# Attention's bias and threshold by one-column operations, gating's factors in PSUM, and the split sums of x in one block

## The chip, the cores and the metric

The kernel runs on one core of one Trainium2 chip. The metric is the device time of one execution in microseconds, the median over several runs. A core has five engines with instruction queues of their own, each worked off in order: TensorE (PE, matmuls), VectorE (DVE), ScalarE (ACT), GpSimd (POOL) and SyncE (SP, which issues most DMAs here). [...] Data lies in SBUF, and matmuls write to PSUM, which has 8 banks.

## The reference

Three computations in a row, all in float32:

```
scores = q @ k.T / 8                        # batch 2, 8 heads, 576 rows, head size 64
scores = where(scores >= max(scores) - tau, scores, -1e9)
attn   = exp(scores - max(scores));  attn /= sum(attn) + 1e-9
x      = attn @ v                           # as 1152 tokens of 512

P = exp(x @ w_gate - max(x @ w_gate))       # 1152 x 8 experts
8 times:  P /= P.sum(1) + 1e-9;  P /= P.sum(0) + 1e-9;  P *= 1152 / 8
x = sum over 8 experts e of  P[:, e] * (relu(x @ w1[e]) @ w2[e])      # hidden size 1024

p = domain_probs / (its row sums + 1e-9)
out = sum over 4 experts e of  p[:, e] * (relu(x @ w1[e]) @ w2[e])
```

The softmax's threshold is taken at the row's own maximum; with `tau` at or above zero the row maximum always stays in.

## The kernel before

**Number format.** Matmuls run on float32 operands that are split in two parts, a rounded `hi` and a remainder `lo`, with three matmuls for one product (lo by hi, hi by lo, hi by hi). A split is one cast on ACT for `hi` and one subtraction on DVE or POOL for `lo`. Splits are done for q, k, v, the weights (names `wh` and `wl`; POOL does the subtraction), x (`xh` and `xl`), the hidden rows (`hh`/`hl`, `hs`) and certain sums of x (`xth` and `xtl`).

**Order.** The program is written out in the order in which each engine is to execute it; the framework adds the semaphores. Three stretches follow each other.

*Attention* (up to some 260 us). 72 units of 128 score rows go through a software pipeline. In one `step`, `scores` of unit t+2 (PE, line 270, 261 for the first ones), `top` of unit t+1 (DVE, row maximum, line 275), `mask` of unit t (DVE, line 287), `guard` (line 291), `line` of unit t+1 (line 279) and `norm` (a reciprocal on DVE, line 295, and a scaling on POOL, line 297) stand in this order; then the transposes of an older unit (PE, line 305), the copy of its transposed rows (ACT, line 312), the exponential of unit t+1 (ACT, line 283), the low part `etl` of the transposed rows (DVE, line 322), and the products with v (PE, lines 340 to 349). `line` makes from the row maximum two columns of the small tile `st`: column 1 is the bias of the exponential, column 2 the threshold of the mask. With m the maximum, `lin` the constants:

```
st[:, 1:3] = lin[:, 0:2] * m - lin[:, 2:4]
lin[:, 0:2] = (-0.125 if tau >= 0 else 0, 1)        lin[:, 2:4] = (0, 8 tau, or a huge number if tau < 0)
```

Between these, PE is given matmuls of the first two experts on the tokens that are ready (`expert_fill`, lines 460 and 488, with DVE's `hl` at line 469 and small copies on POOL). How many of them a step gets is written into the program and does not depend on times.

*Rest of the fill, and gating* (some 260 to 352 us). A loop pulls three pieces of `expert_fill` at a time and between them one piece of a generator: `gate` (lines 709 to 746) at every third turn, and `sums(1)` or `scale` (line 753) in the other turns. `gate` makes the logits, the exponential and then the 8 rounds of normalising `p1`, a tile of 128 rows x 72 numbers (9 token tiles of 8 experts). In a round DVE sums over experts into `rs` (line 731), adds 1e-9 (732), inverts (733) and multiplies `p1` by it (734); PE sums over the rows with a matrix of ones (line 737); DVE sums that over the tiles into `cs` (738), adds, inverts and multiplies (739 to 741). `sums(c)` makes, for one half of the tokens, the sums of column blocks of x that the next layers read (lines 772 to 781) and their splits (line 71 on ACT, line 76 on DVE). Its last six splits go to the tiles `xth` and `xtl`, for which there is room only when the fill's weights are no longer needed; so the generator pauses there.

*The mixtures in half-size blocks* (from 352 us to the end). `layer1` (line 885, 14 slots of six matmuls, ACT and DVE work at lines 860, 861, 890 to 909) and `layer2` (line 989, with the sums into `acc` at line 997) alternate over half experts and halves of the tokens. After each slot `tick` is called: it advances the preparation of the next weights by one piece (`cook1`, `cook2`: a cast on ACT and a subtraction on POOL, at most one every two ticks), and it advances by one piece the first generator of the list `behind`. Whatever remains of a half's generator in `pending` is worked off in `drain`, just before the slots of `layer1` that read `xth` and `xtl` (the fifth slot and on). A slot's matmuls write to a bank that an earlier slot may have filled; the fifth and sixth slot write to those that `s` (line 890) was copied from. After the first `layer1`, `sums(0)` begins, for the other half of the tokens.

PSUM banks of the last two stretches come from one pool of eight, `bank()`.

Of the kernel before, what the change touches and what calls it, by code (L numbers as in the profile page):

```python
# [9 lines left out]
F32 = mybir.dt.float32  # L10
F32R = mybir.dt.float32r
AF = mybir.ActivationFunctionType
ALU = mybir.AluOpType
# [5 lines left out]
E1, E2 = 8, 4  # L19
P = 128  # L20
KT = DM // P
FT = F // P
NT = N // P
# [6 lines left out]
def attention_two_moe_kernel(ctx, tc, qP, kP, qT, kT, vp, tau, wg, w1, w1s, w2, dp, m2w1s, m2w2, out):  # L30
    nc = tc.nc
    V, A, G, T = nc.vector, nc.scalar, nc.gpsimd, nc.tensor
# [4 lines left out]
    def pool(stack, name, bufs=1, **kw):  # L37
        return stack.enter_context(tc.tile_pool(name=name, bufs=bufs, **kw))

    cp = pool(ctx, "const")  # L40
# [13 lines left out]
    tau_sb = cp.tile([P, 1], F32, name="tau_sb")  # L54
    warm = cp.tile([P, 1], F32, name="warm")
    A.activation(warm, ones[:, 0:1], AF.Exp)
    esc = cp.tile([P, 1], F32, name="esc")
    lin = cp.tile([P, 4], F32, name="lin")
    on = cp.tile([P, 1], F32, name="on")
    wg_sb = cp.tile([P, KT, E1], F32, name="wg_sb")  # L60
    wg2 = cp.tile([P, KT, 2 * E1], F32R, name="wg2")
# [7 lines left out]
    def split(eh, el, hi, lo, src):  # L69
        if eh is A:  # L70
            A.copy(hi, src)  # L71
        elif eh is V:
            V.tensor_copy(hi, src)
        else:
            G.tensor_scalar(hi, src, 1.0, 1.0, op0=ALU.mult, op1=ALU.mult)
        el.tensor_tensor(lo, src, f(hi), op=ALU.subtract)  # L76
# [6 lines left out]
    def fetch(n):  # L83
        while len(raws) < n and tiles:
            w, e, ft = tiles.pop(0)
            raw = rp.tile([P, DM], F32, tag="raw", name="raw", bufs=3)
            nc.sync.dma_start(raw, w[e, :, ft])
            raws.append(raw)
# [22 lines left out]
    class Attention:  # L111
# [164 lines left out]

        def line(self, u):
            st = u["st"]
            V.scalar_tensor_tensor(st[:, 1:3], lin[:, 0:2], st[:, 0:1], lin[:, 2:4], op0=ALU.mult, op1=ALU.subtract)  # L279

        def exp(self, u):
            ex = u["ex"] = self.pl.tile([P, 2, HS], F32, tag="ex", name="ex", bufs=4)
# [163 lines left out]
    def bank():  # L446
        return banks.tile([P, 512], F32, tag="mm", name="mm")
# [60 lines left out]
    with ExitStack() as att:  # L508
        ap = pool(att, "attn", side="right")
        ps_s = pool(att, "ps_s", 2, space=PSUM)  # L510
        ps_t = pool(att, "ps_t", 1, space=PSUM)
        ps_r = pool(att, "ps_r", 1, space=PSUM)
        banks.pool = ps = pool(att, "ps_m", 2, space=PSUM)
        at = Attention(ap, ps_s, ps_t, ps_r, ps)
        for p in range(H // 2):
            at.add_pair(0, p, 0, 256, True, p == 0)
        nA0 = len(at.units)
        for p in range(H // 2):
            at.add_pair(0, p, 256, 320, False)
        nA1 = len(at.units)  # L520
        for p in range(H // 2):
            at.add_pair(1, p, 0, S, False)
        at.plan()
        room = [2 * FT]
        at.load()
        G.memset(lin, 0.0)
        G.memset(lin[:, 1:2], 1.0)
        V.tensor_scalar(on, tau_sb, 0.0, None, op0=ALU.is_ge)
        V.tensor_scalar(esc, on, 0.125, None, op0=ALU.mult)
        V.tensor_scalar(lin[:, 0:1], on, -0.125, None, op0=ALU.mult)  # L530
        V.tensor_scalar(on, on, -BIG, BIG, op0=ALU.mult, op1=ALU.add)
        V.scalar_tensor_tensor(lin[:, 3:4], tau_sb, 8.0, on, op0=ALU.mult, op1=ALU.add)

        def side():
            if at.t >= -1:
                fetch(2)
            if at.t >= nA0 - 3 and raws and room[0] and (at.t < nA1 or room[0] > 2 or at.t % 2):
                room[0] -= 1
                cook()
            if at.t == 20:  # L540
                nc.sync.dma_start(wg_sb, wg)
                nc.sync.dma_start(dp_sb, dp)
            if at.t == 24:
                split(V, V, wg2[:, :, :E1], wg2[:, :, E1:], wg_sb)

        def free(n):
            room[0] += n

        X0, X1 = Expert(0), Expert(1)
        near, far = ((0, 0), (1, P)), ((2, 32), (3, 32 + P))  # L550
        todo = [(nA0 + 3, expert_fill(hp, X0, 0, 256, near, acc, None, 0, at.later, keep)),
                (nA1 + 3, expert_fill(hp, X0, 256, 320, far, acc, tail0[0], 0, at.later, free)),
                (nA1 + 3, expert_fill(hp, X1, 0, 256, near, y1, None, 0, at.later, keep)),
                (nA1 + 3, expert_fill(hp, X1, 256, 320, far, y1, tail0[1], 0, at.later, keep))]

        left, spent = [0], [0]

        def pull(n, end=True):

            for i in range(n):  # L560
                if not todo or at.t <= todo[0][0] or (left[0] == 1 and not end):
                    return i
                left[0] = next(todo[0][1], -1)
                if left[0] < 0:
                    todo.pop(0)
                if left[0] <= 0:
                    left[0] = 0
                    return i + 1
            return n

        def fill(phase, busy):
            if phase == 0:
                if 0 <= at.t < nA0 - 3:
                    room[0] -= 1
                    cook(None if at.t % 2 else at.later)
                spent[0] = pull(3)
            elif left[0] or not busy:
                pull(max((RA1 if at.t < nA1 + 3 else RA2) - spent[0], 0), True)

        while at.step(fill, side):  # L580
            pass
        at.flush()
        while left[0]:
            pull(1)
        at.flush()
        while raws:
            cook()
            fetch(2)
# [25 lines left out]
    gp = pool(ctx, "gate", side="right", reuse_waits="tile")  # L614
# [61 lines left out]
    behind = []  # L676
# [26 lines left out]
    def gate():  # L703
        lt = gp.tile([2 * E1, N], F32, name="lt")
        for q in range(4):
            lg = bank()
            for i, x in enumerate((xl, xh)):
                for kt in range(KT):
                    T.matmul(lg[:2 * E1, :HS], lhsT=wg2[:, kt], rhs=x[:, kt, q * HS:(q + 1) * HS],
                             start=i == 0 and kt == 0, stop=i == 1 and kt == KT - 1)  # L710
            A.copy(lt[:, q * 2 * P:(q + 1) * 2 * P], lg[:2 * E1, :2 * P])
            A.copy(lt[:, 8 * P + q * 32:8 * P + (q + 1) * 32], lg[:2 * E1, 2 * P:HS])
            yield 1
        pl = bank()
        for t in range(NT):
            T.matmul(pl[:, t * E1:(t + 1) * E1], lhsT=lt[:, t * P:(t + 1) * P], rhs=both[:2 * E1], start=True, stop=True)
        A.copy(p1.rearrange("p t e -> p (t e)"), pl[:, :NT * E1])
        gm = gp.tile([P, 4], F32, name="gm")
        V.tensor_reduce(gm[:, 0:1], p1, axis=AX.XY, op=ALU.max)
        yield 1  # L720
        pm, pn = bank(), bank()
        T.transpose(pm[:1, :P], gm[:, 0:1], ident)
        V.tensor_reduce(gm[:1, 1:2], pm[:1, :P], axis=AX.X, op=ALU.max)
        yield 1
        T.matmul(pn[:, 0:1], lhsT=ones[:1, :], rhs=gm[:1, 1:2], start=True, stop=True)
        V.tensor_scalar(gm[:, 2:3], pn[:, 0:1], -1.0, None, op0=ALU.mult)
        A.activation(p1, p1, AF.Exp, bias=gm[:, 2:3])
        rs = gp.tile([P, NT], F32, name="rs")
        cs = gp.tile([P, E1], F32, name="cs")
        for _ in range(8):  # L730
            V.tensor_reduce(rs, p1, axis=AX.X, op=ALU.add)
            V.tensor_scalar(rs, rs, 1e-9, None, op0=ALU.add)
            V.reciprocal(rs, rs)
            V.tensor_tensor(p1, p1, rs[:, :, None].to_broadcast([P, NT, E1]), op=ALU.mult)
            yield 1
            pc = bank()
            T.matmul(pc[:, :NT * E1], lhsT=ones, rhs=p1.rearrange("p t e -> p (t e)"), start=True, stop=True)
            V.tensor_reduce(cs, pc[:, :NT * E1].rearrange("p (t e) -> p e t", t=NT), axis=AX.X, op=ALU.add)
            V.tensor_scalar(cs, cs, 1e-9, None, op0=ALU.add)
            V.reciprocal(cs, cs)  # L740
            V.scalar_tensor_tensor(p1, p1, float(N) / E1, cs[:, None, :].to_broadcast([P, NT, E1]),
                                   op0=ALU.mult, op1=ALU.mult)
        V.tensor_reduce(rs, dp_sb, axis=AX.X, op=ALU.add)
        V.tensor_scalar(rs, rs, 1e-9, None, op0=ALU.add)
        V.reciprocal(rs, rs)
        V.tensor_tensor(p2, dp_sb, rs[:, :, None].to_broadcast([P, NT, E2]), op=ALU.mult)
        yield 1
# [55 lines left out]
    gt, s1, sl = gate(), sums(1), scale()  # L803
# [21 lines left out]
    hp = pool(ctx, "hs", reuse_waits="tile")  # L825
    tp = pool(ctx, "temps", reuse_waits="tile")
    pending = [None, s1]
    behind += [s1, gt, sl]

    def begin(c, work):  # L830
        pending[c] = chain(pending[c] or (), work)
# [240 lines left out]
```

## Time and profile before

| | us |
|---|---|
| median of 3 runs | 1394.73 (1394.54 to 1398.56) |
| the profiled execution | 1393.83 |
| its span, from the first to the last instruction | 1392.0 |
| PE busy | 1331.3 (96%) |
| DVE busy | 710.0 (51%) |
| POOL busy | 662.0 (48%) |
| ACT busy | 560.9 (40%) |

Durations come from one profiled execution. A row of the timeline has the start in us from the beginning of the span, the duration in us, engine, line of the program, operation, the tiles that it writes and reads, shapes and the count of merged instructions; in brackets stands the idle time of the engine ahead of it and what ended that time. A matmul's row is longer than its share of PE's time, since the next one starts before it has ended: times of PE are read from start to start. Times of DVE are read in the same way where short operations follow each other.

### The profile page before, as it was taken

The page shows a single profiled execution, that of the slowest core. Times are in us where ns is not written, and L with a number is a line of the kernel's source. Part 1 is how long each engine was busy: PE and PEld are TensorE (multiplying, and loading weights), DVE is VectorE, ACT ScalarE, POOL GpSimd, SP SyncE. Part 2 cuts the span into 40 slices and gives each one's busy share as a digit, 9 for nine tenths or more (in the row PEclk, how much of TensorE's full clock was granted, in tenths as well). Part 3 has the DMA queues.
Part 4 walks back from the last instruction along what each step waited for, and adds up shares of the span by engine and source line. Part 5 has one row for each costly group of instructions (what it writes and reads, how often), then busy time and mean ns, then how long its engine had stood idle before and what let it go on. Part 6 is the DMA issues. An engine that isn't in the chain of part 4 may idle for free.

```text
span 1392.0 us, 21443 instructions
## 1 busy us (share of the span) xinstructions
PE 1331.3 (96%) x8089; PEld 1191.5 (86%) x8089; DVE 710.0 (51%) x1579; ACT 560.9 (40%) x1286; POOL 662.0 (48%) x792
## 2 busy tenths in 40 slices
PE   7788999999889999999999999999899999999998
PEld 4578898889779898988889898988788989888887
DVE  6799999555654333343434343435653434334343
ACT  5767677421444242333323242423442424233331
POOL 5766777351565354345335443542433543453330
PEclk9999999999999999999999999999999999999999
DMA  5522231010221111111111011101011101111101
GB/s 164 154 83 78 77 97 44 24 31 9 72 73 54 46 51 34 54 46 31 54 40 60 24 53 47 58 26 46 24 46 46 61 24 54 46 38 47 31 8 61
DMA packets 42055, 73.61 MB, mean 53 GB/s; under 512 B 5088, under 2 KB 10336, under 8 KB 41952
## 3 DMA queue, kind: packets, MB, share of 16 engines
q1 hardware_dynamic: 41664, 71.96, 17.2%
q8 instruction: 64, 1.05, 0.3%
q14 instruction: 39, 0.32, 0.1%
q10 hardware_dynamic: 288, 0.28, 0.1%
HBM read 69.86 MB, written 2.36 MB: 52 GB/s over the span
## 4 chain that ended last, share of the span: by engine, by line
PE 76%; DVE 14%; ACT 5%; issue 2%; POOL 2%; DMA 0%; DVEq 0%; ACTq 0%; POOLq 0%
PE mm L989 37%; PE mm L885 29%; PE mm L488 4%; DVE ex L287 2%; PE mm L460 2%; DVE st L275 2%; DVE st L279 1%; DVE etl L322 1%; DVE mm L895 1%; ACT wh L71 1%; ACT ex L283 1%; PE pv L340 1%; PE sc L270 1%; ACT hs L860 1%; DVE hs L861 1%
## 5 line engine op out<-in xcount | busy, mean ns | idle before, releaser
L989 PE MATMUL mm<-wh,hs 128*128 128x512 f32 x1344 | 433.2, 395 | 0.0
L76 POOL TENSOR_TENSOR wl<-raw,wh 128x512 fp32r<-128x512 f32 x154 | 200.0, 1304 | 396.6 <-ACT wh L71 379.7
L989 PEld LDWEIGHTS mm<-wh,hs 128*128 128x128 f32 x1344 | 252.3, 188 | 58.0 <-DVE hs L861 0.5
L997 DVE SCALAR_TENSOR_TENSOR acc<-mm,p,acc 128x512 f32<-128x512 f32 x181 | 135.7, 750 | 300.9 <-PE mm L989 300.9
L989 PE MATMUL mm<-wl,hs 128*128 128x512 f32 x672 | 264.5, 394 | 0.0
L890 ACT COPY s<-mm 128x288 f32<-128x288 f32 x84 | 33.7, 402 | 439.4 <-PE mm L885 439.3
L885 PE MATMUL mm<-xh,wl 128*128 128x288 f32 x672 | 147.9, 301 | 16.4 <-ACT u L890 14.3
L861 DVE SCALAR_TENSOR_TENSOR hs<-mm,hs 128x288 fp32r<-128x288 f32 x252 | 111.2, 455 | 86.9 <-ACT hs L860 86.9
L860 ACT ACTIVATE hs<-mm 128x288 fp32r<-128x288 f32 x252 | 98.5, 408 | 132.6 <-DVE mm L895 71.8
L989 PEld LDWEIGHTS mm<-wl,hs 128*128 128x128 f32 x672 | 126.4, 188 | 28.2 <-POOL wl L76 0.4
L885 PE MATMUL mm<-xl,wh 128*128 128x288 f32 x672 | 145.0, 297 | 0.0
L885 PE MATMUL mm<-xh,wh 128*128 128x288 f32 x672 | 144.8, 297 | 0.0
L885 PEld LDWEIGHTS mm<-xh,wl 128*128 128x128 f32 x672 | 110.7, 190 | 25.0 <-ACT u L890 15.7
L76 POOL TENSOR_TENSOR wl<-ws,wh 128x512 fp32r<-128x512 f32 x88 | 114.9, 1309 | 32.6 <-ACT wh L71 32.6
L885 PE MATMUL mm<-xth,wl 128*128 128x288 f32 x504 | 109.2, 298 | 1.7 <-ACT xth L71 1.7
L885 PE MATMUL mm<-xtl,wh 128*128 128x288 f32 x504 | 109.2, 298 | 1.5 <-DVE xtl L76 1.5
L885 PEld LDWEIGHTS mm<-xl,wh 128*128 128x128 f32 x672 | 109.0, 190 | 0.0
L885 PE MATMUL mm<-xth,wh 128*128 128x288 f32 x504 | 108.8, 297 | 0.0
L885 PEld LDWEIGHTS mm<-xh,wh 128*128 128x128 f32 x672 | 108.6, 190 | 0.0
L867 POOL TENSOR_SCALAR ht<-hs 128x128 fp32r<-128x128 f32 x168 | 49.7, 302 | 110.5 <-ACT hs L860 97.9
L71 ACT CAST wh<-raw 128x512 fp32r<-128x512 f32 x154 | 95.3, 619 | 2.2 <-DMA raw<-in_w 0.5
L885 PEld LDWEIGHTS mm<-xtl,wh 128*128 128x128 f32 x504 | 81.8, 190 | 2.0 <-DVE xtl L76 2.0
(167 smaller groups left out, 2383.3 us busy)
## 6 DMA issues: line engine op xcount, KB each, us to landing
raw<-in_w SPq DMA_DIRECT2D x88, 256.0 KB, 2.9
raw<-in_w1s SPq DMA_DIRECT2D x56, 256.0 KB, 2.7
raw<-in_m2w1s SPq DMA_DIRECT2D x32, 256.0 KB, 2.7
raw<-in_m2w SPq DMA_DIRECT2D x32, 256.0 KB, 2.9
kr<-in_kT SPq DMA_DIRECT2D x22, 288.0 KB, 2.9
vr<-in_vp SPq DMA_DIRECT2D x24, 160.0 KB, 2.4
qr<-in_qT SPq DMA_DIRECT2D x8, 288.0 KB, 2.8
out_y<-acc SPq DMA_DIRECT2D x8, 256.0 KB, 2.0
```

What stands on the lines that cost most here:

```text
L71: A.copy(hi, src)
L76: el.tensor_tensor(lo, src, f(hi), op=ALU.subtract)
L275: V.tensor_reduce(st[:, 0:1], u["sc"][:, :, :HS], axis=AX.XY, op=ALU.max)
L287: V.scalar_tensor_tensor(ex, u["sc"][:, :, :HS], st[:, 2:3], ex, op0=ALU.is_ge, op1=ALU.mult, accum_out=st[:, 3:4])
L488: T.matmul(py[:, :256], lhsT=x, rhs=a[:, c0:c0 + 256], start=i == 0, stop=i == 3 * FT - 1)
L860: A.activation(hh, src, AF.Relu)
L861: V.scalar_tensor_tensor(hl, src, 0.0, f(hh), op0=ALU.max, op1=ALU.subtract)
L867: G.tensor_scalar(tail[j][:, :, q:q + 32], f(side[s][j][:, :, 2 * P:]), 1.0, 1.0, op0=ALU.mult, op1=ALU.mult)
L885: T.matmul(m, lhsT=w[:, (2 * g + kt) * P:(2 * g + kt + 1) * P], rhs=operand(u, kt, lo), start=first and j == 0, stop=j == len(ops) - 1, sk ...
L890: A.copy(z[name], m)
L989: T.matmul(py, lhsT=hs[x][:, k, o:o + P], rhs=w, start=n == 0, stop=n == 3 * HF - 1)
L997: V.scalar_tensor_tensor(acc[t], py, s, acc[t], op0=ALU.mult, op1=ALU.add)
```

## The change

Three edits. `line` becomes two operations of one column each, with the per-row constants as their second operand; `lin` has two columns in place of four and is no longer cleared by POOL. The two factor tiles of the gating, `rs` and `cs`, become columns of one PSUM bank that the gating takes from the pool of eight and keeps to its end. What is left of `sums(1)` when the fill ends is issued at once, ahead of the first `layer1`, and is no longer in the list that `tick` works off.

```
-    lin = cp.tile([P, 4], F32, name="lin")
+    lin = cp.tile([P, 2], F32, name="lin")
...
         def line(self, u):
             st = u["st"]
-            V.scalar_tensor_tensor(st[:, 1:3], lin[:, 0:2], st[:, 0:1], lin[:, 2:4], op0=ALU.mult, op1=ALU.subtract)
+            V.tensor_scalar(st[:, 1:2], st[:, 0:1], lin[:, 0:1], None, op0=ALU.mult)
+            V.tensor_scalar(st[:, 2:3], st[:, 0:1], lin[:, 1:2], None, op0=ALU.subtract)
...
-        G.memset(lin, 0.0)
-        G.memset(lin[:, 1:2], 1.0)
...
-        V.scalar_tensor_tensor(lin[:, 3:4], tau_sb, 8.0, on, op0=ALU.mult, op1=ALU.add)
+        V.scalar_tensor_tensor(lin[:, 1:2], tau_sb, 8.0, on, op0=ALU.mult, op1=ALU.add)
...
-        rs = gp.tile([P, NT], F32, name="rs")
-        cs = gp.tile([P, E1], F32, name="cs")
+
+        norms = bank()
+        rs, cs = norms[:, :NT], norms[:, 16:16 + E1]
...
     pending = [None, s1]
-    behind += [s1, gt, sl]
+    for _ in s1:
+        pass
+    behind += [gt, sl]
```

## Rows read from the trace of the kernel before

**Rows 1.** The page: busy time, share of the span and instructions of each engine.
```profile
PE 1331.3 (96%) x8089; PEld 1191.5 (86%) x8089; DVE 710.0 (51%) x1579; ACT 560.9 (40%) x1286; POOL 662.0 (48%) x792
```

**Rows 2.** Two stretches: length, busy us and instructions by engine, granted clock, DMA.
```profile
core 0: us, PE busy (x) PEld busy (x) DVE busy (x) ACT busy (x) POOL busy (x), PEclk, DMA share, GB/s
0.00:145.00 145.00, 119.27 (x722) 94.86 (x722) 117.57 (x311) 95.86 (x183) 91.95 (x111) 0.98 0.40 118
145.00:265.00 120.00, 112.22 (x857) 107.40 (x858) 109.10 (x275) 86.47 (x168) 83.19 (x122) 1.00 0.20 61
```

**Rows 3.** Waits up to 265 us: who for whom, us, times, longest.
```profile
PE et L305 <- DVE etl L322: 12.1, 15, 1.9
...
PE sc L270 <- DVE ex L287: 10.6, 11, 1.4
```

**Rows 4.** Chain of waits up to 265 us, shares by line.
```profile
by line: DVE ex L287 12.6%; DVE st L275 10.1%; PE mm L488 8.2%; DVE st L279 7.5%; DVE etl L322 7.0%; ACT ex L283 5.9%; PE pv L340 5.8%; issue 5.2%; PE sc L270 4.9%; PE et L305 3.8%; DVE eth L325 2.8%; DVE xf L369 2.6%; DVE hl L469 2.4%; PE 
```

**Rows 5.** Lines 279 (busy us, mean ns) and 291 (ns min/median/max).
```profile
L279 DVE SCALAR_TENSOR_TENSOR st<-lin,st 128x2 f32<-128x2 f32 x72 | 37.1, 515 | 0.1
...
L279 DVE SCALAR_TENSOR_TENSOR st<-lin,st x72: 220/472/1323, 6.9 to 251.8; 128x2 f32<-128x2 f32 x72
...
L291 DVE TENSOR_SCALAR st<-st x72: 133/143/154, 9.5 to 253.9; 128x1 f32<-128x1 f32 x72
```

**Rows 6.** Timeline of DVE in one attention step: start us, us.
```profile
151.81 0.14 DVE L291 TENSOR_SCALAR st<-st 128x1 f32<-128x1 f32 x1
151.93 0.53 DVE L279 SCALAR_TENSOR_TENSOR st<-lin,st 128x2 f32<-128x2 f32 x1
152.38 0.15 DVE L295 RECIPROCAL st<-st 128x1 f32<-128x1 f32 x1
152.46 0.66 DVE L322 TENSOR_TENSOR etl<-et,eth 128x512 fp32r<-128x512 f32 x1
```

**Rows 7.** Timeline of PE in the gating, the three rows with a wait.
```profile
300.56 0.41 PE L737 MATMUL mm<-p,ones 128*128 128x72 f32 x2 [0.65 <-DVE p L734]
...
306.11 0.41 PE L737 MATMUL mm<-p,ones 128*128 128x72 f32 x2 [0.79 <-DVE p L734]
...
311.46 0.39 PE L488 MATMUL mm<-wh,hl 128*128 128x256 f32 x1 [0.94 <-DVE hl L469]
```

**Rows 8.** Lines of the gating on DVE: ns min/median/max.
```profile
L732 DVE TENSOR_SCALAR rs<-rs x8: 173/174/896, 293.3 to 327.0; 128x9 f32<-128x9 f32 x8
...
L734 DVE TENSOR_TENSOR p<-p,rs x8: 232/234/1129, 294.4 to 327.5; 128x72 f32<-128x72 f32 x8
...
L726 DVE TENSOR_SCALAR gm<-mm x1: 159/159/159, 292.4 to 292.4; 128x1 f32<-128x1 f32 x1
```

**Rows 9.** Timeline of PE, the first layer 1 and its end.
```profile
352.77 0.42 PE L885 MATMUL mm<-xh,wl 128*128 128x288 f32 x2
...
355.97 0.43 PE L885 MATMUL mm<-xth,wl 128*128 128x288 f32 x2
...
357.23 0.40 PE L885 MATMUL mm<-xtl,wh 128*128 128x288 f32 x1 [0.70 <-DVE xtl L76]
...
360.55 0.40 PE L885 MATMUL mm<-xth,wl 128*128 128x288 f32 x1 [1.74 <-ACT xth L71]
...
361.89 0.61 PE L885 MATMUL mm<-xtl,wh 128*128 128x288 f32 x1 [0.81 <-DVE xtl L76]
362.30 0.68 PE L885 MATMUL mm<-xth,wh 128*128 128x288 f32 x2
...
369.23 0.40 PE L989 MATMUL mm<-wh,hs 128*128 128x512 f32 x1
```

**Rows 10.** Timelines of ACT, DVE and PE around that layer.
```profile
352.97 0.37 ACT L493 COPY acc<-mm 128x256 f32<-128x256 f32 x1 [2.45 <-PE mm L488]
...
360.07 1.10 ACT L71 CAST xth<-xy 128x288 fp32r<-128x288 f32 x3
...
355.85 1.32 DVE L76 TENSOR_TENSOR xtl<-xy,xth 128x288 fp32r<-128x288 f32 x1 [0.82 <-ACT xth L71]
...
358.40 0.45 DVE L76 TENSOR_TENSOR xtl<-xy,xth 128x288 fp32r<-128x288 f32 x1
...
395.20 0.82 PE L885 MATMUL mm<-xh,wl 128*128 128x288 f32 x2 [5.44 <-ACT u L890]
```

## The prediction

> **What bounds the kernel now.** I read the page first: TensorE (PE) is busy 96% of the span and VectorE (DVE) 51% [rows 1]. That is an average over two different kernels. The change touches attention, the gating and the first layers of the first mixture, which are over after some 395 us, so the other views are read for that stretch.
>
> The table by stretches [rows 2] splits the attention stage: in the first 145 us PE is busy 119.27, idle 25.7; in the next 120 us it is idle 7.8. DVE is busy 117.6 and 109.1 of them, so the two nearly tie. The list of waits says which of the two ends last: PE waited 12.1 us for `etl` of DVE (15 times) and 10.6 us for `ex` of DVE (11 times) [rows 3], 22.7 of its 33.5 idle us. The chain of waits up to 265 us agrees: three of its first four lines are DVE's, and line 279, the operation that the change splits, holds 7.5%, which is 19.9 us [rows 4]. That line makes two numbers per row and should be nearly free.
>
> Between 295 and 312 us PE waits three times for DVE, in the gating [rows 7]; between 352 and 395 us it waits for splits of x (`xth`, `xtl`) and once for 5.44 us, when a long stretch of DVE work comes to its end [rows 9, 10].
>
> **The change part by part.** The sums are made against the profiled execution's own 1393.83 us (span 1392.0 and 1.8 around it); the median of the runs shown, 1394.73, is 0.9 above it.
>
> *Attention's line 279.* It runs 72 times, 37.1 us in all, mean 515 ns. Its spread tells why: 220 ns at the least, 1323 at the most, while the one-column tensor_scalar just ahead of it (line 291), in the same 72 places, stays between 133 and 154 [rows 5]. Line 279 reads two tensors from SBUF and GpSimd (POOL) reads SBUF at the same time; the one-column operation with one tensor never pays for that. A DVE operation's successor starts some 80 ns before the row's end (line 279 starts at 151.93, takes 0.53, its successor starts at 152.38 [rows 6]), so line 279 holds the queue 515 - 80 = 435 ns, 31.3 us in all.
>
> In its place stand two one-column tensor_scalars with one tensor each and a per-row factor from SBUF. The trace has none of that exact kind. From below, the slot of a small operation is 0.08 (152.38 to 152.46 [rows 6]); line 291's is 0.12 (151.81 to 151.93); the undisturbed line 279, which also has a per-row factor, holds 220 - 80 = 0.14. I take 0.13 each, 0.26 for both. From above each could wait as line 279 does now: 0.435 each. So per unit 0.435 becomes 0.26 (0.16 to 0.87), and DVE saves 72 x 0.175 = 12.6 us (20 saved to 31 lost).
>
> How much of it reaches the end? 19.9 of the 31.3 us of slots are on the chain, 64%: 8.1 us. Room for it is there, though not everywhere: spread evenly over the 265 us, 6.9 of the 12.6 fall in the first 145, where PE idles 25.7, and 5.7 in the next 120, where PE idles only 7.8 [rows 2], so some of these end at PE. In return the exponential on ScalarE (ACT), queued behind line 279, now needs only the first of the two. I take **-8.0** (-12 to -3.5, without the case in which both operations wait). What is late next: PE itself, then `etl`.
>
> The two memsets that go from POOL's start, and the smaller `lin`, are worth nothing: the first matmul waits for its DMA at the start of the span, which no memset holds up.
>
> [...]
>
> *Gating's factors in PSUM.* In each of 8 rounds, lines 732 and 734 (and 741, like 734) take 0.17 and 0.23 us undisturbed and up to 0.90 and 1.13 when POOL reads SBUF beside them [rows 8], so a disturbed one loses 0.7 to 0.9. With the factors in PSUM, lines 734 and 741 keep one tensor in SBUF, and 732 none, so by the reading above none waits. The cost of reading PSUM: line 726, one column from PSUM, takes 159 ns [rows 8] against 143 for line 291 [rows 5], so +16 ns, six such operations in a round, 0.1 us. PE's waits here are 0.65 + 0.79 + 0.94 = 2.4 us [rows 7]. The first two follow line 734 at once, and one disturbed operation each is as long as they are. The third waits for `hl`, queued on DVE behind a whole round of short dependent operations, which stays; I let it keep nearly all of its 0.94. I take **-1.5** (-2.4 to +0.5). The bank that the factors hold leaves 7 of 8 to the matmuls while the gating lasts; the program has two or three open at once, so none is missed. In the later rounds PE does not wait for DVE, so what they save is free time of DVE.
>
> [...]
>
> *The six splits of x in one block.* Now they are handed out piece by piece behind the first slots of layer 1, and what is left is forced before the slot that first reads them. PE starts that layer at 352.77, and runs its first 24 matmuls to 355.97, 0.133 us each. [...] The layer's 84 matmuls need 84 x 0.133 = 11.2 us and took until 369.23, 16.5. So 5.3 us are lost.
>
> After the change ACT's queue holds: the last `acc` copy, to 353.34, then six `xth` casts at a pitch of some 0.34 us (three take 1.10), to 355.4, and only then the two `s` copies and the weight cast behind them. DVE's six `xtl` run beside this at 0.45 each, as the one at 358.40, slots of 0.37, to about 356.2. The 1.32 us of the one at 355.85 came from POOL's weight split beside it [rows 10]; that split waits for the weight cast, now behind the block. The matmuls that need the first splits come at 355.97: ready. Who waits for the delayed `s` copies: the slot at 355.97 overwrites the bank they read. The first ends at about 355.8, just before. The results of layer 1 then pile up 1 to 2 us on DVE and ACT and catch up before layer 2. Weight casts on ACT and POOL's splits behind them move by the same 2 us; they serve the next layer, 15 us away. The gating and scaling generators that stood behind the splits are spent by then.
>
> Layer 2 could start at 364.0. I allow 0.7 us for the lag of layer 1's results and the tail copies on POOL behind them. The DVE work up to 395.20 [rows 10] starts when layer 1's last result is out, so it moves along, and its 5.44 us stay. I take **-4.6** (-5.3 to 0; if every `xtl` takes 1.3 after all, the last is out at about 361.5, two of the three waits come back and the gain is about 2).
>
> **Sum:** 8.0 + 1.5 + 4.6 = 14.1; 1393.83 - 14.1 = 1379.7, with the 0.9 of the median **1380.5 us**.
>
> **Rivals.**
> 1. *PE takes over in attention.* For: after 145 us PE idles 7.8 of 120 us, 6% [rows 2]. Against: its waits for DVE are 22.7 us. If only 3.5 of the 8 come through: 1385.
> 2. *The block of splits gives its gain back.* Layer 1 ends earlier, but the DVE work up to 395 is not, because DVE's splits meet POOL's and its results lag. For: that work ends last there, with 5.44 us of PE idle [rows 10]. Against: it starts behind layer 1's last result. The 4.6 go: 1385.
> 3. *More than forecast.* The whole 12 us, the gating's 2.4 and the block's 5.3: 1393.83 - 19.7 + 0.9 = 1375, and down to 1373 where a stretch at the lower clock goes as well.
> 4. *Slower: the one-column operations wait for POOL too.* [...] Price: at 0.435 each, 0.87 against 0.435, 31 us of DVE, 64% on the chain, 20; less the 6.1 of the other parts: 1408. At 0.22 each attention saves nothing, and from 0.28 each on the sum of all parts is a loss. For: line 732, a tensor_scalar of nine columns with one tensor, does wait at times [rows 8], and no row shows one column with a factor from SBUF. Against: line 291, one column, never waits [rows 5].
> 5. *The change does not bite.* The operations are shorter, but the units are paced by the exponential, the mask and PE, so attention gains nothing; rival 2 holds as well, and the gating's 1.5 alone come through: 1393.
>
> **Chances.** Forecast 0.56 (own range 1376 to 1385), rival 1 0.17, rival 2 0.10, rival 3 0.08, rival 4 0.05, rival 5 0.04. A measurement of this kernel tells 0.3%, 4.2 us, from no change. The first four cases lie below 1390.5, but the tails of rivals 1 and 2 together reach it: faster 0.89, same 0.06, slower 0.05. The range 1373 to 1390 leaves out rivals 4 and 5 and the ends of the others.
>
> **What would show it.** In the changed profile: the two new lines at 130 to 210 ns with a maximum near their median (a maximum near 1 us means rival 4); PE's idle time up to 265 us down from 33.5 to about 25, its waits for `etl` and `ex` down from 22.7; the gating's lines 732, 734, 741 all under 0.3 us, with at most one PE wait left there; layer 1's first `xtl` and `xth` waits gone, no lower clock right behind them, and layer 2 starting some 11.5 us after layer 1. I am wrong if PE's waits for DVE stay while the new lines are short, or if the 5.44 us before 395 grow by what layer 1 gains.

## The result, and the profile after

The changed kernel takes 1378.2 us (median of 4 runs, 1377.03 to 1380.36) against 1395.01 before (4 runs): ratio 0.9876, 95% interval 0.9855 to 0.9897. Forecast were 1380.5, range 1373 to 1390. The profiled execution after is the slowest of its four, 1380.36 with a span of 1378.5; against the span before of 1392.0 it shows 13.5 of the 16.8 us, and a second profiled execution of the same kernel (e4 below, span 1376.6) shows 15.4.

The page after, same columns as [rows 1]: PE has the same work, DVE 17 us less.

```profile
PE 1329.0 (96%) x8089; PEld 1191.8 (86%) x8089; DVE 692.9 (50%) x1651; ACT 559.1 (41%) x1286; POOL 660.5 (48%) x790
```

The two new lines (279 for the bias, 280 for the threshold) and the old line 291, now 292, in ns min/median/max, stand against [rows 5]:

```profile
L279 DVE TENSOR_SCALAR st<-st,lin x72: 212/214/217, 6.8 to 245.1; 128x1 f32<-128x1 f32 x72
...
L280 DVE TENSOR_SCALAR st<-st,lin x72: 202/204/207, 6.9 to 245.3; 128x1 f32<-128x1 f32 x72
...
L292 DVE TENSOR_SCALAR st<-st x72: 134/143/153, 9.4 to 247.2; 128x1 f32<-128x1 f32 x72
```

Where one operation took 220 to 1323 ns, two take 214 and 204, and neither spreads by more than 5 ns. DVE's timeline in one step, against [rows 6], gives the slots:

```profile
148.79 0.14 DVE L292 TENSOR_SCALAR st<-st 128x1 f32<-128x1 f32 x1
148.91 0.21 DVE L279 TENSOR_SCALAR st<-st,lin 128x1 f32<-128x1 f32 x1
149.04 0.20 DVE L280 TENSOR_SCALAR st<-st,lin 128x1 f32<-128x1 f32 x1
149.16 0.15 DVE L296 RECIPROCAL st<-st 128x1 f32<-128x1 f32 x1
```

From start to start these are 0.13 and 0.12 us: DVE is held 0.25 us in a unit, where line 279 held it 0.435 in the mean.

What line 279 waited for can be seen beside these rows. The long one of [rows 6] (from 151.93, 0.53 us) ends at 152.46, 0.02 us behind an instruction of POOL that had begun before it. In the changed kernel the same instruction of POOL covers both new rows, and they are as short as ever. First before, then after:

```profile
151.00 1.44 POOL L76 TENSOR_TENSOR kl<-kr,kh 128x576 fp32r<-128x576 f32 x1 [0.31 <-ACT kh L71]
```

```profile
147.99 1.45 POOL L76 TENSOR_TENSOR kl<-kr,kh 128x576 fp32r<-128x576 f32 x1 [0.36 <-ACT kh L71]
```

It is so throughout. Before, 41 of the 72 rows of line 279 are longer than 300 ns; each began while POOL was running and ends 8 to 20 ns behind POOL's instruction. After, 46 rows of line 279 and 45 of line 280 lie wholly inside an instruction of POOL, and they take 202 to 217 ns like the others.

Now the three stretches, one by one. Each is bounded by matmuls that stand in both programs, so the same matmuls are compared. Attention is taken from the start to the same point of the fill: before, that is the sum of [rows 2]; after, it ends 6.7 us earlier, with 1579 matmuls in both:

```profile
0.00:258.30 258.30, 231.23 (x1579) 203.77 (x1580) 214.78 (x658) 181.16 (x350) 174.73 (x231) 0.98 0.32 94
```

PE was idle for 33.5 us of the 265 and is now for 27.1; DVE's busy time fell from 226.7 to 214.8. The waits that answer to [rows 3] (lines 270 and 306 of PE, for `ex` and `etl`):

```profile
PE sc L270 <- DVE ex L288: 9.9, 11, 1.4
...
PE et L306 <- DVE etl L323: 7.6, 9, 1.6
```

The wait for `etl` fell by 4.5 us and from 15 times to 9. The one for `ex`, of which 7.8 us lie in the first 65 us, hardly moved. The chain of waits up to 258 us shows who bounds the stage now, against [rows 4]: PE's lines lead, and lines 279 and 280 are no longer among the first twelve.

```profile
by line: PE mm L489 9.4%; PE mm L461 9.2%; DVE ex L288 8.1%; PE sc L270 8.1%; issue 7.4%; PE et L306 6.7%; PE pv L341 6.3%; DVE st L275 6.0%; ACT ex L284 5.7%; PE pv L350 3.7%; PE pv L348 3.2%; DVE etl L323 2.7%; POOL ex L298 1.8%; DVE st L
```

The gating's stretch took 81.0 us before, and 78.5 now. Its lines 732 and 734, against [rows 8], and the whole stretch (length, PE busy and so on):

```profile
L732 DVE TENSOR_SCALAR mm<-mm x8: 174/175/176, 286.9 to 317.9; 128x9 f32<-128x9 f32 x8
...
L734 DVE TENSOR_TENSOR p<-p,mm x8: 229/230/232, 287.3 to 318.3; 128x72 f32<-128x72 f32 x8
```

```profile
265.10:343.50 78.40, 78.36 (x622) 76.36 (x621) 38.42 (x120) 19.36 (x51) 28.31 (x59) 1.00 0.07 22
```

PE is busy for 78.36 of 78.40 us: the three waits of [rows 7] are gone. (In e4, a second execution, 0.17 us of the third is left.)

Layer 1 on PE, against [rows 9], and then ACT and DVE beside it, against [rows 10]:

```profile
343.57 0.43 PE L887 MATMUL mm<-xh,wl 128*128 128x288 f32 x2
...
346.73 0.43 PE L887 MATMUL mm<-xth,wl 128*128 128x288 f32 x2
...
349.86 0.54 PE L887 MATMUL mm<-xh,wl 128*128 128x288 f32 x2 [0.56 <-ACT u L892]
...
355.56 0.39 PE L991 MATMUL mm<-wh,hs 128*128 128x512 f32 x1
...
381.73 0.58 PE L887 MATMUL mm<-xh,wl 128*128 128x288 f32 x1 [5.48 <-ACT u L892]
```

```profile
343.77 0.37 ACT L494 COPY acc<-mm 128x256 f32<-128x256 f32 x1 [2.45 <-PE mm L489]
344.04 2.10 ACT L71 CAST xth<-xy 128x288 fp32r<-128x288 f32 x6
346.04 0.70 ACT L892 COPY s<-mm 128x288 f32<-128x288 f32 x2
...
344.58 2.29 DVE L76 TENSOR_TENSOR xtl<-xy,xth 128x288 fp32r<-128x288 f32 x6
```

Layer 1 takes 355.56 - 343.57 = 12.0 us, before 16.5. The waits for `xth` and `xtl` are gone; there is a new one of 0.56 us for `u`, a copy on ACT that comes late: ACT and DVE both began with the block, and the first results of the layer came behind it. The six `xtl` take 2.29 us, and none meets POOL. The 5.48 us ahead of the second layer 1 stayed to 0.04 us, and from 379.1 to 385.9 us, around the end of that wait, the granted clock was 0.50.

### The profile page after: what moved, and what is told of

The parts are those of the page before. It is cut to its first block, busy times and chain, and to the rows that moved or that the text cites. A ratio compares the mean times of both kernels' runs of the same rounds, so it can differ in the third digit from the quotient of the medians.

```text
span 1378.5 us, 21581 instructions
## 1 busy us (share of the span) xinstructions
PE 1329.0 (96%) x8089; PEld 1191.8 (86%) x8089; DVE 692.9 (50%) x1651; ACT 559.1 (41%) x1286; POOL 660.5 (48%) x790
## 4 chain that ended last, share of the span: by engine, by line
PE 82%; DVE 9%; ACT 5%; issue 2%; POOL 1%; DMA 0%; DVEq 0%; ACTq 0%; POOLq 0%
PE mm L991 37%; PE mm L887 29%; PE mm L489 5%; PE mm L461 4%; DVE ex L288 2%; PE sc L270 2%; DVE mm L897 1%; PE et L306 1%; PE pv L341 1%; DVE st L275 1%; ACT wh L71 1%; ACT ex L284 1%; ACT hs L862 1%; DVE hs L863 1%; PE pv L350 1%
## 5 line engine op out<-in xcount | busy, mean ns | idle before, releaser
L892 ACT COPY s<-mm 128x288 f32<-128x288 f32 x84 | 33.5, 400 | 437.8 <-PE mm L887 437.6
L887 PEld LDWEIGHTS mm<-xh,wl 128*128 128x128 f32 x672 | 110.9, 191 | 25.8 <-ACT u L892 16.5
L625 POOL TENSOR_TENSOR ws<-raw 128x512 f32<-128x512 f32 x44 | 57.3, 1303 | 53.4 <-DMA raw<-in_w1s 31.2
```

What stands on the lines that cost most here:

```text
L625: G.tensor_tensor(s, a, b, op=op)
L887: T.matmul(m, lhsT=w[:, (2 * g + kt) * P:(2 * g + kt + 1) * P], rhs=operand(u, kt, lo), start=first and j == 0, stop=j == len(ops) - 1, sk ...
L892: A.copy(z[name], m)
```

## The experiments

**The three parts, each alone, and all three again.** Each kernel has only the named hunks of the change:

```
e1:  lin of two columns, line() as two tensor_scalars, no memsets
e2:  -        rs = gp.tile([P, NT], F32, name="rs")
     -        cs = gp.tile([P, E1], F32, name="cs")
     +        norms = bank()
     +        rs, cs = norms[:, :NT], norms[:, 16:16 + E1]
e3:  -    behind += [s1, gt, sl]
     +    for _ in s1:
     +        pass
     +    behind += [gt, sl]
e4:  all of it
```

> Only the two one-column operations in attention, gating and the splits of x as before. Theory (line 279 lost its time waiting beside GpSimd, because it reads two tensors from SBUF): the two new lines keep 0.20 to 0.22 us rows with no long ones, attention ends 6 to 8 us earlier, the kernel takes 1387 to 1389 us. The gating keeps its three waits of PE, 2.4 us, unless the shift moves them against POOL. Rival (the three parts need each other: the gain comes only where a later wait goes too): under 3 us, 1392 or more.

> Only the gating's factors in PSUM. Theory: lines 732, 734 and 741 stay at 0.17 to 0.23 us with no row near 1 us, PE's three waits in the gating (2.4 us) go, 1392.5 us. Rival (the waits in the gating went in the changed kernel only because attention's end moved against POOL's splits): the waits stay and the time is within 1 us of before.

> Only the six splits of x in one block ahead of layer 1. Theory: PE's waits of 0.70, 1.74 and 0.81 us go with the stretch at the lower clock behind them, layer 2 starts 4.5 us earlier against the start of layer 1, the 5.4 us before the second layer 1 stay, 1390.5 us. Rival (the gain is given back at the DVE work ahead of the second layer 1): the later wait grows by 3 us or more, time within 1.5 us of before.

> The changed kernel once more, on the chip and beside the runs of the three parts alone. If the parts add up, its gain is the sum of theirs within 2 us: 6.7 + 2.5 + 4.5 = 13.7 by the profiled executions, 1381 us; the medians shown with the result say 16.8, 1378 us. Rival (the parts share a gain, or one opens what another needs): 3 us or more off the sum of the three alone.

| kernel | median us | ratio to before (95%) |
|---|---|---|
| before, beside these | 1396.57 | |
| e1, attention | 1388.90 | 0.9942 (0.9926 to 0.9957) |
| e2, gating | 1392.67 | 0.9972 (0.9960 to 0.9984) |
| e3, block of splits | 1391.28 | 0.9964 (0.9950 to 0.9978) |
| e4, all three | 1378.73 | 0.9869 (0.9852 to 0.9886) |

By the ratios the parts give 0.58, 0.28 and 0.36%, together 1.22%; all three give 1.31%. Each part is faster than before by itself, and within the intervals they add up: both rivals of "they need each other" fall. This rests on the medians: the single profiled execution of before, 1393.83, is faster than 18 of the 19 beside these, and against it alone the profiled executions of e1 to e3 gain 3.6, 0.7 and 2.4 us, and that of e4 15.3.

e1 alone shows why the gating's waits deserved an edit of their own. With attention earlier, the gating's rounds meet POOL at other places, and PE waits longer there than before:

```profile
293.66 0.41 PE L736 MATMUL mm<-p,ones 128*128 128x72 f32 x2 [1.07 <-DVE p L733]
...
301.06 0.41 PE L736 MATMUL mm<-p,ones 128*128 128x72 f32 x2 [2.63 <-DVE p L733]
```

That is 3.7 us against the 2.4 of [rows 7]. Among e1's lines are some that read and write SBUF alone and waited up to 1.3 us (line 738 there is the former 739, eight columns, one tensor):

```profile
L738 DVE TENSOR_SCALAR cs<-cs x8: 171/172/1319, 289.2 to 325.3; 128x8 f32<-128x8 f32 x8
...
L740 DVE SCALAR_TENSOR_TENSOR p<-p,cs x8: 232/234/1153, 290.8 to 325.8; 128x72 f32<-128x72 f32 x8
```

In e2, where attention ends as late as before, the same two kinds of line (733 and 735, for 732 and 734) stay put with the factors in PSUM:

```profile
L733 DVE TENSOR_SCALAR mm<-mm x8: 174/174/176, 293.5 to 324.5; 128x9 f32<-128x9 f32 x8
...
L735 DVE TENSOR_TENSOR p<-p,mm x8: 230/230/232, 293.9 to 325.0; 128x72 f32<-128x72 f32 x8
```

Three of line 733's eight rows and four of line 735's began while an instruction of POOL was running, and none was held. PE waits nowhere in e2's gating; in e3, where the factors are in SBUF, it waits 1.07, 1.52 and 0.17 us. So the waits went because of the place of the factors, not because of a shift. e3's layer 1 takes 12.0 us (353.39 to 365.35), and its later wait, the one that could have taken the gain back, is as long as before:

```profile
391.53 0.82 PE L887 MATMUL mm<-xh,wl 128*128 128x288 f32 x2 [5.46 <-ACT u L892]
```

**What makes a small operation wait.** Each of three kernels is the changed one with one more operation in every unit, behind bias and threshold, its result unused:

```
x1:  V.tensor_scalar(st[:, 6:7], st[:, 0:1], lin[:, 1:2], None, op0=ALU.subtract)
x2:  V.scalar_tensor_tensor(st[:, 6:7], lin[:, 0:1], st[:, 0:1], lin[:, 1:2], op0=ALU.mult, op1=ALU.subtract)
x3:  V.tensor_scalar(st[:, 6:8], lin, st[:, 0:1], None, op0=ALU.mult)
```

> The changed kernel with one more one-column operation like the threshold's in each of the 72 units, its result unused. Theory (what counts in attention is how long DVE's queue is held): its row is 0.20 us, its slot 0.12 to 0.13, DVE is held 9 us longer, and about half of it reaches the end as in the change (13.3 us of DVE gave 6.7): 1382 to 1384. Rival (the gain came from the bias being ready earlier for the exponential, not from DVE's time): the operation stands behind bias and threshold, so under 1.5 us, 1380 or less.

> The changed kernel with one more operation in each unit, one column wide but with two SBUF tensors and a per-row factor, its result unused. Theory (two SBUF tensors wait for GpSimd): rows from 0.21 to about 1.3 us, mean near 0.5 as line 279 before, and the time goes back to near that of the attention before, 1386 to 1390. Rival (the width of two columns made line 279 wait): rows of 0.2 us throughout, time as with one column more, 1382 to 1384.

> The changed kernel with one more tensor_scalar in each unit, two columns wide, with one SBUF tensor and a per-row factor, its result unused. If only the number of SBUF tensors counts: rows of 0.2 us throughout, time as with one column more. If the width counts too (line 732 with nine columns and one tensor waited at times): rows up to 1.3 us, mean near 0.5, time near 1386 to 1390. With this the slower rival of the prediction is measured at its nearest form.

The added line 281 in ns min/median/max, first of x1, then of x2, then of x3:

```profile
L281 DVE TENSOR_SCALAR st<-st,lin x72: 201/204/209, 7.2 to 247.2; 128x1 f32<-128x1 f32 x72
```

```profile
L281 DVE SCALAR_TENSOR_TENSOR st<-lin,st x72: 208/254/1432, 7.0 to 256.9; 128x1 f32<-128x1 f32 x72
```

```profile
L281 DVE TENSOR_SCALAR st<-lin,st x72: 218/278/1417, 7.3 to 257.9; 128x2 f32<-128x2 f32 x72
```

x1 took 1384.60 us (ratio 0.9915, 0.9902 to 0.9929), x2 1393.25 (0.9973, 0.9962 to 0.9983), x3 1393.45 (0.9978, 0.9965 to 0.9991). Neither of my two causes, two tensors or two columns, was the whole. One column with two tensors waited (mean 440 ns), and so did two columns with one tensor (448 ns); only one column with one tensor never did (201 to 209 ns in x1). Ahead of each of them the lines 279 and 280 of the same kernel stay at 0.20 to 0.22 us, so it is the form of the operation and not the place in the step. 26 rows of x2 and 29 of x3 are longer than 300 ns, and each of these ends 7 to 29 ns behind an instruction of POOL.

x1 to x3 also give the price of DVE's time in attention. x1 holds DVE 0.12 us longer in a unit, 9 us, and x2 and x3 0.36 us (440 less 80 ns), 26 us. By the ratios x1 is 0.46% slower than e4, 6.4 us, and x2 and x3 1.04 and 1.09%, 14.5 and 15.2 us; against x4 (below), which ran beside them, it is 4.8, 13.4 and 13.6 us. What of that belongs to attention is seen at the first logits, the matmuls that follow the stage. In e4, x1, x2 and x3:

```profile
263.86 0.69 PE L708 MATMUL mm<-xl,wg 128*16 128x288 f32 x4
...
266.82 0.69 PE L709 MATMUL mm<-xl,wg 128*16 128x288 f32 x4
...
276.53 0.69 PE L709 MATMUL mm<-xl,wg 128*16 128x288 f32 x4
...
277.56 0.69 PE L709 MATMUL mm<-xl,wg 128*16 128x288 f32 x4
```

They come 3.0, 12.7 and 13.7 us later: of DVE's added time about half arrives in x2 and x3, and a third in x1. The same point differs by 2.5 us between executions with the same attention (262.56 in n2, 265.04 in the first profile of the changed kernel), so x1's share is known only roughly. A part of what x1 lost lies behind the stage: from 265 to 300 us its mean granted clock was 0.95, against 1.00 in e4. e4 first, then x1:

```profile
265.00:300.00 35.00, 35.00 (x282) 33.68 (x282) 15.50 (x48) 11.38 (x31) 20.42 (x25) 1.00 0.11 31
...
265.00:300.00 35.00, 35.00 (x266) 33.16 (x265) 11.82 (x38) 11.20 (x31) 17.83 (x29) 0.95 0.10 33
```

x1 came out 0.6 us above my upper expectation and x2 and x3 three above theirs.

**Is it the earlier bias?** The changed kernel with the two lines in the other order:

```
-            V.tensor_scalar(st[:, 1:2], st[:, 0:1], lin[:, 0:1], None, op0=ALU.mult)
             V.tensor_scalar(st[:, 2:3], st[:, 0:1], lin[:, 1:2], None, op0=ALU.subtract)
+            V.tensor_scalar(st[:, 1:2], st[:, 0:1], lin[:, 0:1], None, op0=ALU.mult)
```

> The changed kernel with the threshold computed ahead of the bias. DVE's time is the same; the exponential gets its bias one slot, 0.12 us, later, 72 times 8.9 us at most. Theory (DVE's queue is what counts): within 1.5 us of the changed kernel, 1378 to 1380. Rival (the earlier bias is part of the gain): 2.5 us or more slower, 1381 or more, and ACT's waits for the bias grow.

1379.83 us (ratio 0.9884, 0.9869 to 0.9898): 1.1 us above e4 by the medians and 0.15%, 2.1 us, by the ratios, with intervals that overlap. ACT's waits ahead of the exponential, for DVE's `st`, did grow, from 15.0 us in e4 to 17.7, but the first logits start at 264.41, between the 263.86 and 265.04 of the two executions of the changed kernel. What the earlier bias gives can't be told from nothing here; DVE's time is the cause.

**The wait that stayed, 5.48 us.** Two ways to take DVE's work for the other half of x out of the stretch behind layer 1, and both together. n1 begins `sums(0)` ahead of the first layer 1, together with what may be left of the gating and the scaling. n2 issues the first half of `sums(0)` in the last turns of the fill, where POOL is idle:

```
n1:  -            layer1(i, c)
                  if i == 0:
                      while behind:
                          next(behind[0], None) or behind.pop(0)
                      begin(0, sums(0))
     +            layer1(i, c)
n2:  -            t1, t2, t3, t4 = (new() for _ in range(4))
     +            t1 = new()                  # t2 to t4 likewise, each ahead of its use
     ...
              next(sl, None)
     +        if ahead:                       # 7 times
     +            ahead -= 1
     +            next(s0)                    # s0 = sums(0); the rest begins where it did
n3:  n2, and the rest begun ahead of layer 1
```

> The changed kernel, with sums(0) begun ahead of the first layer 1 in place of behind it. It tests what PE's wait of 5.48 us ahead of the second layer 1 comes from. If from DVE's sums standing in one stretch behind layer 1: 14 of its 24 pieces now lie among layer 1's slots, the wait falls to under 2 us and the lower clock behind it shortens, 1373 to 1376. Rival (the sums delay layer 1's own results by as much): layer 2 starts 3 us or more later, and the time is within 2 us of the changed kernel.

> The changed kernel, with the first half of sums(0) (7 of its 14 sum steps; the tiles are taken one by one for it) issued in the last turns of the fill, where POOL and DVE are idle. DVE has some 5 us less to do behind layer 1: PE's wait of 5.48 us falls to 1 to 2 us, 1373 to 1375. Rival (the wait is not DVE's time but something that starts only with layer 1's end, such as the scaling into acc or the tail copies): it stays above 4 us.

> Both together: half of sums(0) in the fill, the rest begun ahead of the first layer 1. If DVE's time behind layer 1 is the cause, the wait is gone, 1371 to 1374. Rival (the pieces among layer 1's slots cost what they save): 1 us or more slower than the half in the fill alone.

n1 took 1378.99 us (ratio 0.9873, 0.9859 to 0.9888), n2 1376.87 (0.9855, 0.9839 to 0.9872), n3 1379.11 (0.9871, 0.9856 to 0.9886). n1 went as its rival said: the 5.48 us vanished, but layer 2 starts 15.6 us after layer 1 in place of 12.0, since PE waits in layer 1 and at its end instead; the longest of these:

```profile
350.01 0.53 PE L887 MATMUL mm<-xh,wl 128*128 128x288 f32 x2 [1.66 <-ACT u L892]
...
362.25 0.50 PE L991 MATMUL mm<-wh,hs 128*128 128x512 f32 x1 [1.71 <-DVE hs L863]
...
367.68 0.50 PE L991 MATMUL mm<-wh,ht 128*128 128x512 f32 x1 [1.23 <-POOL ht L979]
```

In n2 it fell to 3.19, not to the 1 to 2 that I expected, and what is left on DVE ahead of it still runs beside POOL (two splits in 3.01 us, where six took 2.29 above):

```profile
378.48 0.50 PE L893 MATMUL mm<-xh,wl 128*128 128x288 f32 x2 [3.19 <-ACT u L898]
```

```profile
365.72 3.01 DVE L76 TENSOR_TENSOR xl<-xy,xh 128x288 fp32r<-128x288 f32 x2
```

n3 went as its rival said as well: the wait ahead of the second layer 1 is gone, layer 2 starts 15.4 us after layer 1, and n3 is 2.2 us slower than n2. So that wait is DVE's time, stretched by POOL; work put among layer 1's slots moves it there, and of these three only n2, which put work where DVE has room, shortened it without that price. n2 has the lowest median of all kernels here, 1.9 us below e4. In its profile the second layer 1 takes 16.1 us (369.57 to 385.68) against 18.5 in e4 (369.48 to 387.98), which is the shorter wait; but its attention, in which nothing was changed, happened to be 1.3 us shorter too. The intervals overlap, so that n2 beats the changed kernel is likely, not shown.

## Why the prediction was right

Direction, size and all three mechanisms held; each part alone gained, and its waits went as laid down. Term by term, in times of the profiled executions:

- *Attention, -8.0.* The first logits (line 709, after it 708), which follow it in both programs, start at 265.0 after and at 263.9 in e4, against 271.7: -6.7 and -7.9. e1 alone gives -7.6, and by its ratio 0.58% of 1396.57, 8.1 us. The slot of 0.26 for both operations measured 0.25, and DVE's saving was 13.3 us for my 12.6. The share that arrives (I read 64% from the chain) is 50 to 60%. The two errors go against each other, so that -8.0 came out so close is in part luck. Where the rest stayed is, as I read it, the stage's first part, since PE's waits for `ex` went from 10.6 to 9.9 us only; no run tests that. That rival 1 (PE takes over) would cut the gain to 3.5 did not happen, but its sign is there: PE leads the chain now.
- *Gating, -1.5.* The stretch went from 81.0 to 78.5 us, -2.5. The step that failed is the third wait, for `hl` behind a round of short operations. I let it keep nearly all of its 0.94 us, since that round stays; it is gone, with 0.17 us left in e4. By the order on DVE I put that down to the operations ahead of it, which no longer wait; no run tests it by itself, and in e3, which kept the factors in SBUF, this wait is 0.17 us too, behind two longer ones. PSUM's price was small, as I had read it, and smaller still: line 732 takes 175 ns for 174 and line 734 230 for 234; the inversion, line 733, took 227 against 215, which is under my +16 too.
- *Block of splits, -4.6.* -4.5 (12.0 for 16.5). The queue of ACT came out as laid down: the block's casts took 2.10 us behind the `acc` copy, the `s` copies followed at 2.5 us after the layer's start, in time for the slot that overwrites their bank. I allowed 0.7 us for the lag; 0.56 of it showed as the wait for `u`. The clock: over that layer (343.5 to 355.5 us) the granted clock was 1.00, where before it was 0.50 from 361.4 to 364.8 us and a pair of matmuls took 0.68 [rows 9].
- *Rival 2* fell: the wait ahead of the second layer 1 stayed at 5.4 to 5.5 us and moved with layer 1 in every run but those that moved DVE's sums.
- *Rival 4* fell: with one column and one tensor, a per-row factor did not make the operation wait (lines 279 and 280, 202 to 217 ns). The row that spoke for it, line 732, was right about something else, the width: two columns with one tensor waited (x3, mean 448 ns, up to 1417), and one such operation more in a unit took 1.09 of the change's 1.31%. A change with two columns in one of its halves was not run.
- *Rivals 3 and 5:* the gating gave its whole 2.4 us, as rival 3 had it, the other two parts no more than their forecast; e1's gain shows that attention is not paced by the rest alone, as rival 5 had it.
- The sum of the three was 14.1, and the profiled executions show 13.5 and 15.4. The medians show 16.8 and 17.8. What they show beyond that is the spread of the executions: that of before with the profile lies 1.2 us under the median of its runs and 2.7 under the median beside e4, and that of the changed kernel 2.2 above its own. In these runs the spread goes with the clock: the 19 executions of before beside e1 to e4 took from 1392.22 us, at a mean granted clock of 0.993, to 1399.67, at 0.985. I can't assign these 2 to 3 us to a part of the change.

## What to carry to other kernels

Look at the spread of a small operation and not at its mean: a row that took 220 ns at best and 1.3 us at worst, next to a neighbour that never spread, waited here for something that its form brought with it; the other engines' rows beside it showed for what. Two one-column operations of a form that didn't wait (202 to 217 ns) beat one that did (mean 515 ns), and one operand in PSUM kept operations that need two tensors from waiting (230 to 232 ns in e2, line 735, for up to 1129 before). How much of an engine's saved time reaches the end can be estimated from its share of the chain of waits, but with care: the chain said 64%, the change gave 50 to 60%, and the added operations cost a third to a half.

## What the runs showed of the hardware

I had not expected the line to be so sharp: a tensor_scalar of two columns with a single SBUF tensor waited beside POOL (x3, 218 to 1417 ns), and one of one column did not (x1 and the changed kernel, 201 to 217 ns, also inside a running instruction of POOL in the changed kernel). The held rows of line 279 before ended 8 to 20 ns behind POOL's instruction. And a source and target in PSUM cost the gating's short DVE operations next to nothing: 175 ns for 174 at nine columns, 12 ns more for an inversion.
